# Windowed attention and a feed-forward network on one core: attention's matrix products in groups, values two pairs behind, a fourth buffer of weights

## The chip, the cores and the metric

The kernel runs on one core of a Trainium2 chip. The metric is the time of one execution in microseconds on the device. Before the change it is 954.46 us, the median of three runs (952.74 to 955.82).

## What is computed

The inputs are q, k and v (8 batches, 8 heads, 576 positions, 64 columns a head) and two weight matrices (512 x 2048 and 2048 x 512), all float32. Each head attends to the last 128 positions with a bias that falls linearly with the distance; then a two-layer network runs over all 4608 tokens:

```
scores = q @ k^T / 8 + slope_h * (-|i - j|),  masked to 0 <= i - j < 128
attn   = softmax(scores);  x = attn @ v          # 4608 x 512 after the heads are joined
h = x @ w_in                                      # 4608 x 2048
g = h if h >= 1, 0 if h <= -1, else (h + 1)^2 / 4
out = g @ w_out                                   # 4608 x 512
```

## The kernel before

The 4608 tokens are cut into 12 chunks of 384 (three blocks of 128). A *pair* is two heads of one chunk, so a chunk has four pairs and the program 48 (`p` = 0 to 47). The first two chunks of attention (pairs 0 to 7) run in float32. From pair 8 on (`p8`) every operand is split into a high and a low float16 half, and each product is made of three: high x high, high x low, low x high.

**Scores of a pair** (`scores_of_pair`, L451). The two heads lie on partitions 0 to 63 and 64 to 127, so a score product uses half the rows of the array (64*128 in the profile), and the two heads' products alternate. Blocks 0 and 1 together are 12 products into two PSUM banks, one for each head; block 2 is a second call with 6 products into two more banks. All of attention shares three banks (`ps_a`). `soften` (L467) then takes the bias and the row minimum on VectorE (L484) and the exponential on ScalarE (L486).

**Weights.** `weights_t` (L507) scales and splits the softmax of one head into float16 (`hl`, L531 and L532) and transposes it with a DMA on the queue of SyncE (L533) into `lu`, which has three buffers.

**Values of a pair** (`values_of_pair`, L558). 24 products (18 in the chunks that begin a batch) multiply `lu` with the split v (`vs`). Each head fills half the output columns (128*64 in the profile). The sum lies in one of the three banks and is split into `xh` on ScalarE (L580) and `xl` on VectorE (L581).

**Feed-forward.** For each of 16 slices of the hidden layer, `layer1` (L597) makes 12 products of 384 columns into one of two banks (`ps_h`). The gate `g` is made on ScalarE and in two halves on VectorE (L607 to L609), then split (`gh` on ScalarE, L616; `gl` on GpSimd, L617). `layer2` (L620) makes 9 products of 512 columns two slices later. These use the whole array (128*128).

**What sets the order.** `segments` (L655 to L724) lists the steps of attention; `emit_attention` (L728) gives them out in step with the slices of the feed-forward of the chunk before, so that attention of chunk c + 1 runs under the feed-forward of chunk c. A scheduler then places each instruction on its engine at build time by priority and by when it holds its inputs ready; each engine runs its list in that order. `behind` (L240) fixes that a step stands after given instructions of its engine: the products of one call are chained with it, but others may stand between them. In the loop from L698, pair p's scores (blocks 0 and 1), scores (block 2), values of pair p - 1, and weights of pair p follow one another.

Of the kernel before, what the change touches and what calls it, by code (L numbers as in the profile page):

```python
# [8 lines left out]
F32 = mybir.dt.float32  # L9
F16 = mybir.dt.float16  # L10
# [10 lines left out]
def windowed_attention_then_ffn(  # L21
# [26 lines left out]
    P = 128  # L48
# [3 lines left out]
    NQB = 3  # L52
    CH = NQB * P
    NCHUNK = NT // CH
    NP = NCHUNK * NPAIR
# [5 lines left out]
    X = mybir.AxisListType.X  # L61

    LIGHT = 2

    const = ctx.enter_context(tc.tile_pool(name="const", bufs=1))
    wp = ctx.enter_context(tc.tile_pool(name="wp", bufs=1))
# [2 lines left out]
    ap1 = ctx.enter_context(tc.tile_pool(name="ap1", bufs=1))  # L69
# [170 lines left out]
    def behind(instructions, f):  # L240

        with ExitStack() as stack:
            for i in instructions:
                stack.enter_context(tc.issue_after(i))
            f()


    pair = {}
    head = {}
    xn = {}  # L250
# [2 lines left out]
    softened, scored_at = {}, {}  # L253
    lo_rows = [slice(0, D), slice(D, P)]
# [5 lines left out]

    late = []
    vns = {}

    def load_first(p):

        n = f"_{p}"
        if p < 2:
            qr = ap1.tile([P, CH], F32, name="qr" + n, tag=("qr", "ql")[p])
        else:
            if p == 2:  # L270
                late.append(wp.tile([P, 2, CH], F32, name="qr_23", tag="wo5"))
            qr = late[0][:, p - 2]
        kr = k_0[p // 2][:, p % 2]
        pair[p] = dict(qr=qr, ql=qr, kr=kr)
        DMA.dma_start(qr, q[p * P:(p + 1) * P, :CH])
        DMA.dma_start(kr, k[p * P:(p + 1) * P, :CH])

    def load_qk(p):

        c, g = divmod(p, NPAIR)  # L280
        if c == 0 or c >= LIGHT:
            return
        n = CH + before(c) * P
        st = pair.setdefault(p, {})
        qr = st["qr"] = ap1.tile([P, CH], F32, name=f"qr_{p}", tag="qr")
        DMA.dma_start(qr, q[g * P:(g + 1) * P, c * CH:(c + 1) * CH])
        kr = st["kr"] = ap1.tile([P, CH + P], F32, name=f"kr_{p}", tag=("kl", "kk")[p % 2])
        DMA.dma_start(kr[:, :n], k[g * P:(g + 1) * P, (c + 1) * CH - n:(c + 1) * CH])
# [127 lines left out]

    def prepare_q(p):
        if p >= NPAIR:
            ql = pair[p]["ql"] = ap1.tile([P, CH], F32, name=f"ql_{p}", tag="ql")
            S.activation(ql, pair[p]["qr"], AF.Copy, scale=qscale[:, p % NPAIR:p % NPAIR + 1])  # L420

    def split_v(p):
# [28 lines left out]
    def scores_of_pair(p, blks):  # L451
        c = p // NPAIR
        t = pair[p]["h"]
        pts = [bank(f"s_{2 * p + j}_{blks[0]}").rearrange("r (m w) -> r m w", w=2 * P) for j in range(2)]
        last = []
        for n, i in enumerate(blks):
            c0, k0 = window(c, i)
            for s, (a, b) in enumerate(((0, 0), (0, 1), (1, 0))):
                for j, r in ((1, lo_rows[1]), (0, lo_rows[0])):
                    behind(last, lambda: last.append(  # L460
                        T.matmul(pts[j][:, n, c0:], t[r, a, i * P:(i + 1) * P], t[r, b, CH + k0:CH + k0 + 2 * P - c0],  # L461
                                 start=(s == 0), stop=(s == 2)).ins))
                    last = last[-1:]
        for j in range(2):
            softened[p] = soften(2 * p + j, blks, pts[j])

# [40 lines left out]
    def weights_t(m):  # L507

        ep = head[m]["ep"]
        if m < LIGHT * H:  # L510
            pt = bank(f"p_{m}")[:, :CH].rearrange("r (i w) -> r i w", w=P)
            for i in range(NQB):
                T.transpose(pt[:, i, :], ep[:, i, :], ident)
            lu = head[m]["lu"] = ap1.tile([P, 2 * NQB, P], F32, name=f"lu_{m}", tag="lu", bufs=3)
            own = lu[:, 1::2, :]
            ga = S.copy(own, pt)
            G.affine_select(out=lu[:, 0::2, :], in_=own, pattern=[[0, NQB], [-1, P]],
                            base=0, channel_multiplier=1, compare_op=ALU.is_gt, fill=0.0)
            gg = G.affine_select(out=own, in_=own, pattern=[[0, NQB], [1, P]],
                                 base=0, channel_multiplier=-1, compare_op=ALU.is_ge, fill=0.0)  # L520
            done_t[m] = [head[m]["held"].ins, ga.ins, gg.ins]
            return
        lu = head[m]["lu"] = ap1.tile([P, 2, 2 * NQB, P], F16, name=f"lu_{m}", tag="lu", bufs=3)
        hl = ap1.tile([P, 2, NQB, 2 * P], F16, name=f"hl_{m}", tag="ep", bufs=2)
        z, rc = head[m]["z"], head[m]["rc"]
        lone = 1 - before(m // H)
        if lone:
            G.memset(hl[:, :, 0, :P], 0.0)
        for i in range(NQB):
            c0 = P if i < lone else 0  # L530
            S.activation(hl[:, 0, i, c0:], z[:, i, c0:], AF.Copy, scale=rc[:, i:i + 1])  # L531
            V.scalar_tensor_tensor(hl[:, 1, i, c0:], z[:, i, c0:], rc[:, i:i + 1], hl[:, 0, i, c0:], ALU.mult, ALU.subtract)  # L532
        DMA.dma_start(lu.rearrange("p s i w -> p (s i) w"), hl.rearrange("p s i w -> p (s i w)"), transpose=True)  # L533
# [24 lines left out]
    def values_of_pair(p):  # L558
        c, g = divmod(p, NPAIR)
# [2 lines left out]
        lus = [head.pop(2 * p + j)["lu"] for j in range(2)]  # L562
        px = bank(f"x_{p}")[:, :CH]
        todo = [(i, a, b) for i in [*range(NQB), -1] if i + b0 >= 0 for a, b in ((0, 0), (0, 1), (1, 0))]
        last = []
        for n, (i, a, b) in enumerate(todo):
            q0, q1 = max(i, 0), min(i + 2, NQB)
            first = 2 * i + 1 if i >= 0 else 0
            for j, r in enumerate(lo_rows):
                behind(last, lambda: last.append(  # L570
                    T.matmul(px[r, q0 * P:q1 * P], vs[:, a, i + b0, r], lus[j][:, b, first:first + q1 - q0, :].rearrange("p a w -> p (a w)"),  # L571
                             start=(n == 0), stop=(n == len(todo) - 1), skip_group_check=True).ins))
                last = last[-1:]
# [81 lines left out]
    segments = []  # L655
    ready = [0]
    turned = {}
    M1 = LIGHT * H
    p8 = M1 // 2
# [38 lines left out]
    for p in range(p8, NP):  # L698
        c, g = divmod(p, NPAIR)
        nc_, ng = divmod(p + 5, NPAIR)  # L700
        new = p + 5 < NP
        segments.append([lambda p=p: scores_of_pair(p, (0, 1))])
        if p == p8:
            segments.append([lambda p=p: behind(softened[p], lambda: reach_of(p + 4))])
        if new:
# [4 lines left out]
        if g == NPAIR - 1 and c + 1 < NCHUNK:  # L710
            segments.append([lambda c=c: near_of(c + 1)])
        segments.append([lambda p=p: split_v(p)] + ([lambda p=p: load_all(p + 6)] if p + 6 < NP else []))
        if p > p8:
            segments.append([lambda p=p: values_of_pair(p - 1)])
            if g == 0:
                ready.append(len(segments))
# [3 lines left out]
        if p + 1 < NP:  # L720
            segments.append([lambda p=p: split_qk(p + 1)])
        segments.append([lambda p=p: weights_t(2 * p + 1)])
    segments.append([lambda: values_of_pair(NP - 1)])
    ready.append(len(segments))  # L724
    assert len(ready) == NCHUNK + 1
    at = [0]
# [94 lines left out]
    for i, ops in enumerate(ffn):  # L821
        c, r = divmod(i, STEPS)
# [37 lines left out]
```

## Time and profile before

| | |
|---|---|
| median of three runs | 954.46 us (952.74 to 955.82) |
| the profiled execution | 954.13 us |
| its span, first to last instruction | 952.4 us |
| mean granted TensorE clock | 0.988 of full speed |
| TensorE busy | 932.2 us, 98% |
| VectorE busy | 707.2 us, 74% |
| ScalarE busy | 662.6 us, 70% |
| GpSimd busy | 231.3 us, 24% |
| chain of work that ended last | TensorE 88%, VectorE 5%, ScalarE 4% |

PE in the profile is TensorE's matrix products, PEld its loading of the stationary operand, DVE VectorE, ACT ScalarE, POOL GpSimd and SP SyncE. Products are pipelined: the next starts before the last one has ended, so the distance from start to start tells what a product costs, and the length of a row does not. A row of the timeline with "x12" is twelve instructions of one line that follow one another without others between.

### The profile page before, as it was taken

How to read it: one execution, taken by the hardware profiler on the slowest of the kernel's cores; microseconds unless marked ns; L12 is line 12 of the kernel's file. 1: busy time of each engine (PE TensorE's matmuls, PEld its weight loads, DVE VectorE, ACT ScalarE, POOL GpSimd, SP SyncE). 2: the span in 40 equal slices, each digit the busy share in tenths (PEclk: the TensorE clock that was granted, in tenths of full speed). 3: DMA queues.
4: the chain of work that ended last, by engine and by line, in shares of the span. 5: the costliest groups of instructions: out<-in, count | busy, mean ns of one | idle time of the engine just before them, and what ended most of it. 6: DMA issues, size and time to landing. Idle time of an engine off the chain costs nothing.

```text
span 952.4 us, 17560 instructions
## 1 busy us (share of the span) xinstructions
PE 932.2 (98%) x5941; PEld 488.6 (51%) x5941; DVE 707.2 (74%) x2073; ACT 662.6 (70%) x1668; POOL 231.3 (24%) x328
## 2 busy tenths in 40 slices
PE   8889999999999999999999999999999999999997
PEld 6434554455555555555555555555555555455553
DVE  7799979998877877877877877876786777655332
ACT  6788958888678678667667767766866766655332
POOL 5332311121322222222222222122222221221221
PEclk9699999999999999999999999999999999999999
DMA  8557722535435434633532532443433212411000
GB/s 260 190 189 262 230 62 74 86 87 141 85 67 123 84 59 112 113 65 95 111 85 61 126 81 65 112 93 84 107 88 66 67 35 41 93 34 34 34 1 33
DMA packets 178730, 91.32 MB, mean 96 GB/s; under 512 B 128848, under 2 KB 168016, under 8 KB 178640
## 3 DMA queue, kind: packets, MB, share of 16 engines
q1 hardware_dynamic: 178496, 90.07, 38.8%
q8 instruction: 46, 0.75, 0.3%
q14 instruction: 44, 0.36, 0.1%
q10 hardware_dynamic: 144, 0.13, 0.0%
HBM read 49.28 MB, written 9.44 MB: 62 GB/s over the span
## 4 chain that ended last, share of the span: by engine, by line
PE 88%; DVE 5%; ACT 4%; DMA 1%; issue 1%; POOL 0%; SPq 0%; DVEq 0%; ACTq 0%; POOLq 0%
PE h L600 13%; PE acc L632 12%; PE h L601 12%; PE h L602 12%; PE acc L634 12%; PE acc L633 12%; PE s L461 5%; PE x L571 4%; PE acc L629 2%; PE s L445 1%; PE x L548 1%; ACT z L486 1%; DMA vn<-in_v_dram 1%; ACT raw L183 1%; PE idle L88 1%
## 5 line engine op out<-in xcount | busy, mean ns | idle before, releaser
L617 POOL TENSOR_TENSOR gl<-g,gh 128x384 f16<-128x384 f32 x176 | 175.3, 996 | 553.6 <-ACT gh L616 506.6
L608 DVE SCALAR_TENSOR_TENSOR g<-u,half 128x384 f32<-128x384 f32 x176 | 113.6, 646 | 156.6 <-ACT u L607 151.0
L632 PE MATMUL acc<-wo,gh 128*128 128x512 f16 x528 | 200.9, 380 | 0.0
L633 PE MATMUL acc<-wo,gh 128*128 128x512 f16 x528 | 200.2, 379 | 0.0
L634 PE MATMUL acc<-wo,gl 128*128 128x512 f16 x528 | 198.6, 379 | 0.0
L616 ACT CAST gh<-g 128x384 f16<-128x384 f32 x176 | 89.3, 507 | 149.6 <-DVE g L609 126.7
L486 ACT ACTIVATE z<-z,nmax 128x256 f32<-128x256 f32 (+2 forms) x288 | 137.7, 479 | 37.6 <-DVE nmax L484 36.5
L607 ACT ACTIVATE u<-h,shift,fall 128x384 f32<-128x384 f32 x176 | 116.6, 663 | 59.2 <-PE h L602 58.5
L600 PE MATMUL h<-xh,wi 128*128 128x384 f16 x384 | 125.4, 327 | 1.1 <-DVE g L609 1.1
L600 PE MATMUL h<-x,wi 128*128 128x384 f16 x384 | 125.7, 327 | 0.4 <-DVE r L406 0.4
L601 PE MATMUL h<-x,wi 128*128 128x384 f16 x384 | 125.2, 326 | 0.0
L601 PE MATMUL h<-xl,wi 128*128 128x384 f16 x384 | 125.2, 326 | 0.0
L602 PE MATMUL h<-x,wi 128*128 128x384 f16 x384 | 125.2, 326 | 0.0
L602 PE MATMUL h<-xh,wi 128*128 128x384 f16 x384 | 124.9, 326 | 0.0
L484 DVE CUSTOM_DVE_ANT_0 z<-s,near,z_of 128x256 f32<-128x256 f32 (+2 forms) x240 | 98.9, 459 | 23.7 <-PE s L461 23.4
L609 DVE SCALAR_TENSOR_TENSOR g<-h,gain,g 128x384 f32<-128x384 f32 x176 | 108.1, 614 | 3.0
L532 DVE SCALAR_TENSOR_TENSOR hl<-z,rc,hl 128x256 f16<-128x256 f32 (+1 forms) x240 | 104.4, 492 | 7.8 <-ACT hl L531 7.6
L600 PEld LDWEIGHTS <-wi 128*128 128x128 f16 x768 | 74.9, 98 | 64.5 <-issue 11.7
L601 PEld LDWEIGHTS <-wi 128*128 128x128 f16 x768 | 75.2, 98 | 52.2 <-issue 3.7
L602 PEld LDWEIGHTS <-wi 128*128 128x128 f16 x768 | 75.1, 98 | 49.9 <-DVE g L608 0.2
L531 ACT ACTIVATE hl<-z,rc 128x256 f16<-128x256 f32 (+1 forms) x240 | 98.1, 488 | 3.5 <-DVE rc L496 2.9
L634 PEld LDWEIGHTS <-gl 128*128 128x128 f16 x528 | 51.6, 98 | 63.4 <-issue 1.9
(150 smaller groups left out, 1212.0 us busy)
## 6 DMA issues: line engine op xcount, KB each, us to landing
out_dram<-o SPq DMA_DIRECT2D x35, 256.0 KB, 2.8
raw<-in_moe_w_in_dram SPq DMA_DIRECT2D x16, 512.0 KB, 4.1
raw<-in_moe_w_out_dram SPq DMA_DIRECT2D x16, 512.0 KB, 5.0
vn<-in_v_dram SPq DMA_DIRECT2D x32, 256.0 KB, 3.4
qk<-in_q_dram SPq DMA_DIRECT2D x40, 192.0 KB, 2.4
qk<-in_k_dram SPq DMA_DIRECT2D x28, 256.0 KB, 2.9
vn<-in_v_dram SPq DMA_DIRECT2D x16, 192.0 KB, 3.0
qk<-in_k_dram SPq DMA_DIRECT2D x12, 192.0 KB, 2.8
```

What stands on the lines that cost most here:

```text
L486: b = S.activation(z[:, i, c0:], z[:, i, c0:], AF.Exp, bias=nmax[:, i:i + 1], scale=-1.0, accum_out=sm[:, i, 0:1])
L532: V.scalar_tensor_tensor(hl[:, 1, i, c0:], z[:, i, c0:], rc[:, i:i + 1], hl[:, 0, i, c0:], ALU.mult, ALU.subtract)
L600: T.matmul(ph, wi[fc][:, 0, cc, :], xh, start=(cc == 0), stop=False)
L601: T.matmul(ph, wi[fc][:, 0, cc, :], xl, start=False, stop=False)
L602: T.matmul(ph, wi[fc][:, 1, cc, :], xh, start=False, stop=(cc == NCC - 1))
L607: first = S.activation(u, ph, AF.Relu, bias=shift[c] if c else quarter, scale=fall[c][:, col])
L608: V.scalar_tensor_tensor(g, u, half[c] if c else 0.5, u, ALU.min, ALU.mult)
L609: last = V.scalar_tensor_tensor(g, ph, gain[c][:, col] if c else fall[c][:, col], g, ALU.mult, ALU.max)
L617: G.tensor_tensor(gl, g, gh, ALU.subtract)
L632: T.matmul(a, gh[:, ts], wo[fc][:, 0], start=first, stop=False)
L633: T.matmul(a, gh[:, ts], wo[fc][:, 1], start=False, stop=False)
L634: T.matmul(a, gl[:, ts], wo[fc][:, 0], start=False, stop=last)
```

## The change

From pair 8 on, all products of one call of `scores_of_pair` and `values_of_pair` but the first get a raised priority (`held`). For block 2 the order of the two heads is turned round. From pair 14 on (`TIED`) the values of pair p - 2 stand directly behind the scores (blocks 0 and 1) of pair p and are chained to them; until then values follow their pair by one, as before. `lu` gets a fourth buffer, in the place of the two float32 buffers of q of the early pairs, which become the halves of one tile (`q2`). The count of instructions on each engine is the same.

```diff
+    TIED = 14
...
+    def held(last, f):
+
+        if not last:
+            return f()
+        with tc.high_priority(offset=3000):
+            behind(last, f)
+
...
+    q2 = ap1.tile([P, 2, CH], F32, name="q2", tag="q2")
...
-            qr = ap1.tile([P, CH], F32, name="qr" + n, tag=("qr", "ql")[p])
+            qr = q2[:, p]
...
-        qr = st["qr"] = ap1.tile([P, CH], F32, name=f"qr_{p}", tag="qr")
+        qr = st["qr"] = q2[:, 0]
...
-            ql = pair[p]["ql"] = ap1.tile([P, CH], F32, name=f"ql_{p}", tag="ql")
+            ql = pair[p]["ql"] = q2[:, 1]
...
-                for j, r in ((1, lo_rows[1]), (0, lo_rows[0])):
-                    behind(last, lambda: last.append(
+                for j, r in (((1, lo_rows[1]), (0, lo_rows[0])) if blks[0] == 0 else ((0, lo_rows[0]), (1, lo_rows[1]))):
+                    held(last, lambda: last.append(
...
+        if blks[0] == 0 and p >= TIED:
+            scored_at[p] = last[0]
...
-        lu = head[m]["lu"] = ap1.tile([P, 2, 2 * NQB, P], F16, name=f"lu_{m}", tag="lu", bufs=3)
+        n = m % 4
+        lu = head[m]["lu"] = ap1.tile([P, 2, 2 * NQB, P], F16, name=f"lu_{m}", tag="q2") if n == 3 else \
+            ap1.tile([P, 2, 2 * NQB, P], F16, name=f"lu_{m}", tag="lu", bufs=3)
...
-        last = []
+        last = [scored_at[p + 2]] if p + 2 in scored_at else []
...
-                behind(last, lambda: last.append(
+                held(last, lambda: last.append(
...
         segments.append([lambda p=p: scores_of_pair(p, (0, 1))])
+        if p >= TIED:
+            segments.append([lambda p=p: values_of_pair(p - 2)])
+            if g == 1:
+                ready.append(len(segments))
...
-        if p > p8:
+        if p8 < p < TIED - 1:
             segments.append([lambda p=p: values_of_pair(p - 1)])
...
-    segments.append([lambda: values_of_pair(NP - 1)])
+    segments += [[lambda: values_of_pair(NP - 2)], [lambda: values_of_pair(NP - 1)]]
```

What the built programs make of it is shown at three places of pair 23 and the feed-forward of chunk 4. Names end in a running number of the build, which differs between the two programs.

On TensorE before, one product of the scores of block 2 (`s_47_2`, the pair's second head) stands between the two layers of the feed-forward (`h_4_9` is a slice of the first, `acc_4_0` a sum of the second):

```order
L602 LDWEIGHTS wi9_1085
L602 MATMUL h_4_9_5230<-x_4_3_4593,wi9_1085 128x384
L461 LDWEIGHTS h_23_5159
L461 MATMUL s_47_2_5259<-h_23_5159 128x256
L632 LDWEIGHTS gh_4_7_5137
L632 MATMUL acc_4_0_4852<-wo3_2056,gh_4_7_5137 128x512
```

The other five stand 12 products of the feed-forward later. On TensorE after the change the six stand in one piece; these are the last two of them, and the first product behind:

```order
L470 LDWEIGHTS h_23_5050
L470 MATMUL s_46_2_5196<-h_23_5050 128x256
L470 LDWEIGHTS h_23_5050
L470 MATMUL s_47_2_5197<-h_23_5050 128x256
L613 LDWEIGHTS wi8_1006
L613 MATMUL h_4_8_5214<-x_4_0_3910,wi8_1006 128x384
```

The lone product of the pair's third block is gone from its place.

On TensorE before, the values of pair 22 (`x_22`) begin behind the second layer (`acc_4_2`):

```order
L633 MATMUL acc_4_2_4854<-wo4_2218,gh_4_8_5182 128x512
L634 LDWEIGHTS gl_4_8_5183
L634 MATMUL acc_4_2_4854<-wo4_2218,gl_4_8_5183 128x512
L571 LDWEIGHTS vs_22_5039
L571 MATMUL x_22_5324<-lu_44_5141,vs_22_5039 64x256
```

On TensorE after, the values of pair 21 begin behind the twelfth score of pair 23:

```order
L470 MATMUL s_47_0_5096<-h_23_5050 128x256
L470 LDWEIGHTS h_23_5050
L470 MATMUL s_46_0_5095<-h_23_5050 128x256
L584 LDWEIGHTS vs_21_4714
L584 MATMUL x_21_5130<-lu_42_4743,vs_21_4714 64x256
L584 LDWEIGHTS vs_21_4714
L584 MATMUL x_21_5130<-lu_43_4788,vs_21_4714 64x256
```

The values moved from a place of their own in the feed-forward to the end of the scores of the pair two later.

On VectorE before, the passes over the scores of pair 23 (`z_46`, `z_47`) stand behind both halves of the gate of slices 7 and 8 (`g_4_7`, `g_4_8`):

```order
L609 SCALAR_TENSOR_TENSOR g_4_7_5133<-h_4_7_5119,gain4_4638,g_4_7_5133 128x384
L608 SCALAR_TENSOR_TENSOR g_4_8_5178<-u_4_8_5177,half4_4640 128x384
L609 SCALAR_TENSOR_TENSOR g_4_8_5178<-h_4_8_5164,gain4_4638,g_4_8_5178 128x384
L484 ISA z_46_5218,nmax_46_5219<-s_46_0_5204,near_125,z_of5_4134 128x256
L484 ISA nmax_46_5219 128x1
L484 ISA z_46_5218,nmax_46_5219<-s_46_0_5204,near_125,z_of5_4134 128x256
```

On VectorE after, the two passes of the first head stand between the halves of one gate, that of slice 6 (`g_4_6`):

```order
L621 SCALAR_TENSOR_TENSOR g_4_6_5087<-u_4_6_5086,half4_4674 128x384
L495 ISA z_46_5109,nmax_46_5110<-s_46_0_5095,near_125,z_of5_4026 128x256
L495 ISA nmax_46_5110 128x1
L495 ISA z_46_5109,nmax_46_5110<-s_46_0_5095,near_125,z_of5_4026 128x256
L495 ISA nmax_46_5110 128x1
L622 SCALAR_TENSOR_TENSOR g_4_6_5087<-h_4_6_5073,gain4_4672,g_4_6_5087 128x384
```

The second half of the gate moved behind scores that it does not need.

## Rows read from the trace of the kernel before

**Rows 1.** Page, table of engines: busy us, share of the span, instructions.

```profile
PE 932.2 (98%) x5941; PEld 488.6 (51%) x5941; DVE 707.2 (74%) x2073; ACT 662.6 (70%) x1668; POOL 231.3 (24%) x328
```

**Rows 2.** Table by stretch: stretch, its length, busy us of each engine, clock, DMA.

```profile
core 0: us, PE busy (x) PEld busy (x) DVE busy (x) ACT busy (x) POOL busy (x), PEclk, DMA share, GB/s
...
166.00:250.00 84.00, 82.41 (x585) 43.06 (x584) 75.99 (x227) 71.82 (x193) 18.37 (x24) 1.00 0.46 98
250.00:560.00 310.00, 310.00 (x2082) 161.89 (x2081) 239.62 (x699) 220.16 (x580) 73.86 (x93) 1.00 0.43 91
```

**Rows 3.** Waits from 166 us on: who for whom; total us, times, longest.

```profile
PEld L461 <- issue: 44.8, 120, 0.4
...
PE x L571 <- DMA lu<-hl: 1.6, 1, 1.6
```

**Rows 4.** Timeline of TensorE, one score alone: start us, length us, instructions.

```profile
400.21 0.38 PE L633 MATMUL acc<-wo,gh 128*128 128x512 f16 x1
...
401.72 0.38 PE L634 MATMUL acc<-wo,gl 128*128 128x512 f16 x1
402.03 0.28 PE L461 MATMUL s<-h 64*128 64x256 f16 x1
...
402.42 0.33 PE L601 MATMUL h<-x,wi 128*128 128x384 f16 x1
...
404.04 0.33 PE L602 MATMUL h<-x,wi 128*128 128x384 f16 x1
```

**Rows 5.** Timeline of TensorE, five scores.

```profile
411.22 0.33 PE L600 MATMUL h<-x,wi 128*128 128x384 f16 x1
...
411.80 0.50 PE L461 MATMUL s<-h 64*128 64x256 f16 x5
...
412.41 0.33 PE L601 MATMUL h<-x,wi 128*128 128x384 f16 x1
```

**Rows 6.** Timeline of TensorE, six scores.

```profile
242.67 0.33 PE L602 MATMUL h<-x,wi 128*128 128x384 f16 x1
242.93 0.50 PE L461 MATMUL s<-h 64*128 64x256 f16 x6
...
243.59 0.38 PE L633 MATMUL acc<-wo,gh 128*128 128x512 f16 x1
```

**Rows 7.** Timeline of TensorE, the 24 value products of a pair.

```profile
415.43 0.38 PE L634 MATMUL acc<-wo,gl 128*128 128x512 f16 x1
415.74 1.18 PE L571 MATMUL x<-lu,vs 128*64 128x256 f16 x24
...
417.03 0.33 PE L601 MATMUL h<-x,wi 128*128 128x384 f16 x1
```

**Rows 8.** Timeline of TensorE, five scores and 24 values behind them.

```profile
210.64 0.38 PE L633 MATMUL acc<-wo,gh 128*128 128x512 f16 x1
210.95 0.50 PE L461 MATMUL s<-h 64*128 64x256 f16 x5
211.38 1.18 PE L571 MATMUL x<-lu,vs 128*64 128x256 f16 x24
...
212.72 0.38 PE L632 MATMUL acc<-wo,gh 128*128 128x512 f16 x1
```

**Rows 9.** Timeline of all engines, a gate's end and the passes over scores.

```profile
405.89 0.62 DVE L609 SCALAR_TENSOR_TENSOR g<-h,gain,g 128x384 f32<-128x384 f32 x1
...
407.00 0.34 PE L600 MATMUL h<-x,wi 128*128 128x384 f16 x1
...
408.32 0.48 DVE L484 CUSTOM_DVE_ANT_0 z<-s,near,z_of 128x256 f32<-128x256 f32 x1
```

**Rows 10.** Timeline of all engines, the tightest bank of the first layer.

```profile
235.72 0.60 DVE L609 SCALAR_TENSOR_TENSOR g<-h,gain,g 128x384 f32<-128x384 f32 x1
...
236.78 0.34 PE L600 MATMUL h<-x,wi 128*128 128x384 f16 x1
```

## Prediction

> **What bounds the kernel now.** I read the page's table of engines first: TensorE is busy 98% of the span, VectorE 74% [rows 1]. A busy share alone does not say that TensorE is the limit, so the table by stretch came next. From 250 to 560 us TensorE is busy 310.00 of 310.00 us at a granted clock of 1.00 (the 2.4 GHz level), while VectorE has nearly a quarter of its time free; in 166 to 250 us VectorE is busy 75.99 of 84 us, so that is the stretch where it could become late [rows 2]. The waits come third: after 166 us TensorE waited once for data, 1.6 us [rows 3].
>
> The Trainium skill (Perfetto Trace Analysis, Identifying the Most-Contended Engine) speaks against stopping here: matmul busy time is a poor measure because matmuls overlap, and the share of weight loading, 51% here, should judge. By it VectorE would be the engine to relieve. That is the first rival below.
>
> So I read the timeline of single products. Eight 512-column products start from 400.21 to 401.72, seven steps of 0.216 us; 384-column ones start from 402.42 to 404.04, ten steps of 0.162 us [rows 4]. Nothing waits between them. Time is lost only where attention's products, on half the array, stand among those of the feed-forward. I call such a stretch a visit and price it as the time from the start of the product before it to the start of the second product after it, less the plain steps of those two:
> - one score product alone: 402.42 - 401.72 = 0.70, less 0.216 and 0.162: 0.32 us [rows 4];
> - five scores: 412.41 - 411.22 = 1.19, less four steps of 0.162: 0.54 us [rows 5];
> - six scores: 243.59 - 242.67 = 0.92, less 0.378: 0.54 us [rows 6];
> - 24 value products: 417.03 - 415.43 = 1.60, less 0.378: 1.22 us [rows 7];
> - five scores and 24 values in one visit: 212.72 - 210.64 = 2.08, less 0.432: 1.65 us [rows 8].
>
> Five and six cost the same, because scores run in twos, one head on each half of the rows, and an odd one pays for its missing partner. So a visit has a fixed price of about 0.21 us (0.32 less one step of 0.11 for a pair), and a lone score pays the fixed price and an empty half.
>
> **The change part by part.** The same products are issued; their places change. I counted the visits in the built order of TensorE, from pair 8 on (all f16 products of attention).
>
> *Scores held together* (`held`): runs of scores fall from 126 to 87, lone ones from 43 to 6. Joining 1 and 5 into 6 saves 0.32 + 0.54 - 0.54 = 0.32 us; some blocks have 192 or 128 columns and save a little less, so I take 0.31. 39 x 0.31 = 12.1 us. Bounds: the fixed price alone, 39 x 0.21 = 8.2; every lone visit whole, 39 x 0.32 = 12.5.
>
> *Values held together*: runs fall from 46 to 41. I price a split like that of a lone score: 5 x 0.32 = 1.6 us (bounds 1.0 and 1.6).
>
> *Values of pair p-2 directly behind the scores of pair p*: seams between scores and values rise from 3 to 34. A seam saves 0.54 + 1.22 - 1.65 = 0.11 us [rows 5, 7, 8]; 31 x 0.11 = 3.4 us. Bounds: nothing, if the turn from row halves to column halves costs as much as leaving and coming back; 31 x 0.21 = 6.5, if it costs nothing. The one such seam in rows 8 is the same pair of forms, so I take its value.
>
> *Order of the two heads in the third block, one tile for both halves of q*: no instruction more; the copy that reads `q2` has the same readers and the same wait as before. Nothing; if the loads of pairs 4 to 7 came later it would show before 166 us, as at most tenths of a us.
>
> *Fourth buffer of weights*: values of p-2 run while the weights of p-1 are already there, so four are alive. The slot is the old place of q, free after pair 7. The transposing DMAs on SP keep their order and their number; each waits for a buffer whose reader now stands earlier in the pair than the next writer. Nothing. If that cover goes, TensorE waits as it did once at the first values, 1.6 us [rows 3].
>
> *Values one pair later*: the first layer of a chunk needs all four pairs. In chunks 5, 6 and 8 the built order leaves 98 rows between the last values and the first layer, against 62 to 64 before, and the end of the program keeps its 62 rows. No wait.
>
> *Stall terms.* From 250 us on the first layer's banks come free long before they are wanted: the gate ends at 405.89 + 0.62 = 406.51, and the group that reuses its bank starts at 411.22, 4.7 us of room [rows 5, 9]. The tightest place is at 236.78, where the gate ended at 235.72 + 0.60 = 236.32, 0.46 us earlier [rows 10]. There, pairs 8 to 13, the order changes too: one more 0.60 us pass of VectorE ahead of a gate would cost 0.14 us, five of them 2.5. I put the stretch at 0 to 3 us and take 0; the wait of 1.6 us may also go.
>
> Sum: 12.1 + 1.6 + 3.4 = 17.1 us. The profiled run took 954.13 us, 1.7 more than its span of 952.4: 954.13 - 17.1 = 937.0. The median of the three runs is 0.33 us above the profiled one, so I forecast 937.3 us.
>
> **The rivals.**
>
> *TensorE is not the limit.* If busy time misleads, VectorE sets the pace and the moved products only open gaps: 954 us. For it: 74% on VectorE, over 90% in 166 to 250 [rows 1, 2]. Against it: the plain steps have no room for a hidden wait [rows 4]. The rule of the Trainium skill quoted above is not borne out by these rows.
>
> *The three banks become the wait.* A joined visit takes all three banks that attention has: two for scores, the third for values. If one is not yet empty at each of the 32 joined visits, and TensorE waits 0.3 us there, 9.6 us of the gain go: 947 us. For it: the Trainium skill (TensorEngine Tiling, PSUM Bottleneck) warns that packing the array speeds up TensorE but not the emptying of its banks. Against it: of the scores that end at 407.00 the fourth pass of VectorE ends at 408.32 + 0.48 = 408.80 [rows 9], 1.8 us later, while the next visit stands 42 products later, 24 x 0.162 + 18 x 0.216 = 7.8 us.
>
> *The gate falls behind the scores: slower.* VectorE's order now has two passes over the scores between the two halves of a gate (`g_4_6`), so that the gate, and the bank of the first layer, hang on the scores of the visit. It ends about 2 x 0.41 + 0.62 = 1.4 us after the scores instead of before them. Where a first-layer group on that bank follows the visit directly, TensorE waits up to 1.4 us. The gain is eaten from 17.1 / 1.4 = 12 such places on, and at 20 of the 32 the time is 937.3 + 28 = 965 us. For it: the new rows on VectorE. Against it: in the place shown, the group on that bank (`h_4_8`) stands 42 products later, and the room is 4.7 us today [rows 5, 9].
>
> *The order built is not the order meant.* It is partly so: six lone scores and five runs of five stay, and the counts above have them in.
>
> **How the numbers follow.** The forecast has 0.84, the banks 0.08, TensorE not the limit 0.04, the gate behind the scores 0.04. The forecast's own range: the fast end is 937.3 less the 1.6 us wait less the 1.7 us by which the fastest run lies under the median, 934.0; the slow end is 937.3 plus 3 us of the tight stretch, plus 1.4 us of run to run spread, plus the 3.4 us if a seam saves nothing, 945.1. What lies beyond is the banks at 947 and the two rivals behind them, 0.16 in all. Range 934 to 945. A difference under 0.3% (2.9 us) is no change that can be told here. Faster 0.92 (forecast and banks), same 0.04, slower 0.04.
>
> **What would show it.** In the profile after: the score line's busy runs in 12s and 6s with no lone ones from pair 14 on; a joined visit of 12 and 24 costs about 1.98 us (0.87 for twelve scores at six steps of 0.11 and 0.21 fixed, plus 1.22, less 0.11); the weight loads of the scores wait for issue about a third less often than 120 times [rows 3]; TensorE's busy time falls by some 17 us and VectorE's stays within 2 us. Wrong would be: any wait of TensorE for VectorE or for a transposed tile that repeats once a pair after 250 us; a joined visit of over 2.1 us; or an end of the first-chunk stretch that is later than before.

## The result, and the profile after

The changed kernel takes 939.62 us (median of four runs, 938.58 to 942.24), the kernel before beside it 955.14 us (952.74 to 957.36). The ratio is 0.9842, with a 95% interval of 0.981 to 0.9874: 15.5 us faster, against 17.1 forecast. The profiled execution took 939.68 us, 14.5 less than that of before, with a span of 938.0 us. Most of the distance to the forecast is one term, that of the stalls. Executions of one kernel differ by up to 4 us, and the mean granted clock with them (the changed kernel has 0.993 at 938.58 us, 0.987 at 942.24), so that no cause is read from 1 or 2 us between medians.

The page's table of engines after the change [rows 1]:

```profile
PE 917.6 (98%) x5941; PEld 493.1 (53%) x5941; DVE 718.9 (77%) x2073; ACT 660.6 (70%) x1668; POOL 223.6 (24%) x328
```

TensorE is busy 14.6 us less, with the same 5941 products, and its share is 98% as before. That share could not have told beforehand that there was anything to gain. VectorE is busy 11.7 us more.

The table by stretch [rows 2], columns as there:

```profile
166.00:250.00 84.00, 81.16 (x589) 43.20 (x587) 78.48 (x232) 70.59 (x190) 17.63 (x24) 1.00 0.46 104
250.00:560.00 310.00, 310.00 (x2141) 167.30 (x2140) 253.44 (x724) 230.59 (x613) 71.30 (x95) 1.00 0.41 93
```

In 250 to 560 us TensorE still has no idle time, and does 2141 products where it did 2082. In 166 to 250 us it is idle 2.84 us, 1.25 more than before, and VectorE is busy 78.48 of 84. The gain is made in the first kind of stretch, the loss in the second.

The waits from 166 us on [rows 3]: who for whom, total us, times, longest.

```profile
PEld L470 <- issue: 30.9, 78, 0.4
...
PE h L613 <- DVE tt L343: 1.8, 1, 1.8
...
PE h L613 <- DVE half L419: 0.6, 1, 0.6
...
PE x L584 <- DVE nmax L495: 0.2, 1, 0.2
```

Score weights wait for issue 78 times instead of 120, about a third less. The one wait for a transposed tile is gone; three for VectorE are new, and none of them repeats once a pair.

A joined visit in the timeline of TensorE (start us, length us, instructions) [rows 5, 7, 8]:

```profile
392.93 0.33 PE L614 MATMUL h<-x,wi 128*128 128x384 f16 x1
393.10 0.33 PE L615 MATMUL h<-x,wi 128*128 128x384 f16 x1
393.35 0.83 PE L470 MATMUL s<-h 64*128 64x256 f16 x12
394.11 1.18 PE L584 MATMUL x<-lu,vs 128*64 128x256 f16 x24
395.23 0.39 PE L645 MATMUL acc<-wo,gh 128*128 128x512 f16 x1
395.45 0.38 PE L646 MATMUL acc<-wo,gh 128*128 128x512 f16 x1
```

It costs 395.45 - 393.10 = 2.35, less 0.162 and 0.216: 1.97 us, where 1.98 was predicted. After 250 us there are 22 visits of 12 and 24, all at 1.98 us but the four that have narrower scores (1.82 us). No lone score is left there (37 before): all of the third blocks, 33 in number, stand as six, at 0.54 us as in [rows 6] (0.46 where they are narrower).

I priced every visit of both traces from 166 us on as the prediction does. Before there are 163 and after 88. Measured by their starts they sum to 113.9 and 99.1 us; by the prices (fixed, per pair of products, per seam, by each visit's own widths) they should sum to 112.6 and 95.5, a difference of 17.1 as predicted. What the sum after has beyond the prices, about 3.5 us, stands at a few places between 209 and 248 us; before, the one wait of 1.6 us stands beyond them. Without these waits the measured sums are 112.3 and 95.6, a difference of 16.7. The two spans differ by 14.4: the visits with their waits give 14.8, and the first float16 score starts 0.6 us later than before (143.84, 143.23).

The largest of them, in the timeline of VectorE and TensorE, at the place that answers to the tight one [rows 10] (in brackets: idle time just before, and what ended it):

```profile
235.91 0.61 DVE L621 SCALAR_TENSOR_TENSOR g<-u,half 128x384 f32<-128x384 f32 x1
...
236.44 0.55 DVE L594 SCALAR_TENSOR_TENSOR xl<-x,xh 128x384 f16<-128x384 f32 x1
...
236.75 0.77 PE L470 MATMUL s<-h 64*128 64x256 f16 x6
...
236.91 0.34 DVE L495 CUSTOM_DVE_ANT_0 z<-s,near,z_of 128x128 f32<-128x128 f32 x1
...
237.17 0.47 DVE L495 CUSTOM_DVE_ANT_0 z<-s,near,z_of 128x256 f32<-128x256 f32 x1
...
237.58 0.67 DVE L396 TENSOR_REDUCE rows<-vn 128x1 f32<-128x512 f32 x1
...
238.18 0.60 DVE L437 SCALAR_TENSOR_TENSOR vs<-vn,s,vs 128x384 f16<-128x384 f32 x1
...
238.70 0.60 DVE L622 SCALAR_TENSOR_TENSOR g<-h,gain,g 128x384 f32<-128x384 f32 x1
...
239.36 0.32 PE L613 MATMUL h<-x,wi 128*128 128x384 f16 x1 [1.84 <-DVE tt L343]
```

Between the two halves of one gate (235.91 and 238.70) stand five other passes, two of them over scores; before the change only the split of the values (`xl`) stood there. VectorE works without a gap from 235.12 us on, so the gate waits for no score here: it stands in a queue. Only when the second half has read its bank can the first layer go on, at 239.36. The waiting instruction is put down to the short `tt` pass, but the gate's end at 239.30 is what it needed. The visit in front of it, at 236.75, comes to 2.16 us over its price, and 1.84 of it is this wait.

The second place is a lone score with a wait of 0.60 us behind it. A gate's second half and the first layer's product behind the visit, before and after:

```profile
221.42 0.61 DVE L609 SCALAR_TENSOR_TENSOR g<-h,gain,g 128x384 f32<-128x384 f32 x1
...
222.81 0.34 PE L600 MATMUL h<-x,wi 128*128 128x384 f16 x1
```

```profile
221.93 0.61 DVE L622 SCALAR_TENSOR_TENSOR g<-h,gain,g 128x384 f32<-128x384 f32 x1
...
222.59 0.32 PE L613 MATMUL h<-x,wi 128*128 128x384 f16 x1 [0.60 <-DVE half L419]
```

The same three passes stand between the halves in both kernels. Before, the gate ended 0.78 us ahead of the product; after, it ends 0.5 us later, while the score in front of the product starts 0.9 us earlier (221.71, 222.60). TensorE came ahead of a VectorE that had not become faster.

At neither place does the gate hang on the scores of a visit, as in the rival. Passes over scores stand between the halves of 21 of the 171 gates from 166 us on before the change, and of 6 after it; behind one of the six TensorE waits, the one at 235.91. The place of pair 23 that the section on the change shows is among the six, and no sign of what the change does to most gates.

### The profile page after: what moved, and what is told of

The parts are those of the page before. It is cut to its first block, busy times and chain, and to the rows that moved or that the text cites. A ratio compares the mean times of both kernels' runs of the same rounds, so it can differ in the third digit from the quotient of the medians.

```text
span 938.0 us, 17601 instructions
## 1 busy us (share of the span) xinstructions
PE 917.6 (98%) x5941; PEld 493.1 (53%) x5941; DVE 718.9 (77%) x2073; ACT 660.6 (70%) x1668; POOL 223.6 (24%) x328
## 4 chain that ended last, share of the span: by engine, by line
PE 82%; DVE 10%; ACT 5%; issue 1%; DMA 1%; POOL 0%; SPq 0%; ACTq 0%; DVEq 0%; POOLq 0%
PE h L613 12%; PE h L614 12%; PE h L615 12%; PE acc L645 11%; PE acc L646 11%; PE acc L647 11%; PE x L584 4%; PE s L470 4%; PE acc L642 3%; ACT z L497 1%; DVE z L495 1%; PE s L454 1%; DVE g L621 1%; PE x L561 1%; DVE g L622 1%
## 5 line engine op out<-in xcount | busy, mean ns | idle before, releaser
L630 POOL TENSOR_TENSOR gl<-g,gh 128x384 f16<-128x384 f32 x176 | 166.9, 948 | 528.1 <-ACT gh L629 495.0
L621 DVE SCALAR_TENSOR_TENSOR g<-u,half 128x384 f32<-128x384 f32 x176 | 113.6, 645 | 139.9 <-ACT u L620 137.9
L545 DVE SCALAR_TENSOR_TENSOR hl<-z,rc,hl 128x256 f16<-128x256 f32 (+1 forms) x240 | 115.9, 533 | 5.3 <-ACT hl L544 5.2
L495 DVE CUSTOM_DVE_ANT_0 z<-s,near,z_of 128x256 f32<-128x256 f32 (+2 forms) x240 | 98.9, 458 | 14.4 <-PE s L470 14.2
```

The source lines that it names most:

```text
L621: V.scalar_tensor_tensor(g, u, half[c] if c else 0.5, u, ALU.min, ALU.mult)
L630: G.tensor_tensor(gl, g, gh, ALU.subtract)
```

## The experiments

"By price" below is the summed price of all visits in a kernel's built order, less that of before. Each ratio is to the kernel before, run beside it on the same chip (medians 953.93 to 954.40 us).

**held_alone: the kernel before with `held` and nothing else.**

```diff
-                    behind(last, lambda: last.append(
+                    held(last, lambda: last.append(
...
-                behind(last, lambda: last.append(
+                held(last, lambda: last.append(
```

> Before, plus the raised priority inside a call of scores and values, and nothing else (values stay one pair behind, three buffers, heads in the old order). The price theory (TensorE is the limit, and what counts is visits in the built order at the prices of rows 4 to 8): the built order has 142 visits instead of 169 and their summed price falls from 116.2 to 107.6 us, so 955.1 - 8.6 = 946.5 us (945 to 948.5). The prediction's own split of the sum, which gave all joined scores and values to the raised priority: 955.1 - 12.1 - 1.6 = 941.4 us. The rival that VectorE sets the pace: 955 us, no change.

Measured: 945.33 us against 954.12, ratio 0.9912 (0.9891 to 0.9933). That is 8.8 us, as by price, and not the 13.7 that the prediction credits to its two `held` terms. After 250 us the trace still has 15 third blocks cut into one and five scores. The wait for the transposed tile is still there:

```profile
PE x L578 <- DMA lu<-hl: 1.7, 1, 1.7
```

**tie_alone: the changed kernel with `behind` in the place of `held`.**

```diff
-                    held(last, lambda: last.append(
+                    behind(last, lambda: last.append(
...
-                held(last, lambda: last.append(
+                behind(last, lambda: last.append(
```

> The changed kernel without the raised priority (products of a call are only chained, as before); values two pairs behind and chained to the scores, fourth buffer. Price theory: 157 visits in the built order, 11 seams, summed price 112.3 us against 116.2: 955.1 - 3.9 = 951.2 us (949.5 to 953). If the place of the values alone brought the gain, whatever the visits: near 940. If neither part does anything alone: 955.

Measured: 950.19 us, ratio 0.9964 (0.9951 to 0.9976), 3.9 us less than before and as by price. Its trace has 2.6 us of waits between 205 and 238 us, inside visits or directly behind them, 1.0 us more than before has. After 250 us 12 lone scores are left in it.

**lag_untied: values of p - 2, held together, but at the old place and not chained to the scores.**

```diff
-        last = [scored_at[p + 2]] if p + 2 in scored_at else []
+        last = []
...
-        if p >= TIED:
-            segments.append([lambda p=p: values_of_pair(p - 2)])
...
+        if p >= TIED:
+            segments.append([lambda p=p: values_of_pair(p - 2)])
```

> The changed kernel, but the values of pair p-2 keep the place in the pair that values had before and are not chained to the scores (lag of two pairs, four buffers, raised priority stay). Price theory: 148 visits, summed price 110.0 us against 116.2 before and 99.1 changed: 955.1 - 6.1 = 949.0 us (947.5 to 951). The prediction's own split, in which the tie is worth the 31 seams alone: 939.6 + 3.4 = 943.0 us.

Measured: 950.66 us, ratio 0.9958 (0.9944 to 0.9972). That is 3.5 us less than before, where the price says 6.1; its trace has some 3 us of waits, nearly as much as the changed kernel, and before has 1.6. Holding together and standing two pairs behind give less together than holding alone gives (8.8). From here to the changed kernel it is 11 us, which the place directly behind the scores and the chain to them bring; this run does not tell the two apart.

**three_buffers: the changed kernel with three buffers of weights.**

```diff
-        n = m % 4
-        lu = head[m]["lu"] = ap1.tile([P, 2, 2 * NQB, P], F16, name=f"lu_{m}", tag="q2") if n == 3 else \
-            ap1.tile([P, 2, 2 * NQB, P], F16, name=f"lu_{m}", tag="lu", bufs=3)
+        lu = head[m]["lu"] = ap1.tile([P, 2, 2 * NQB, P], F16, name=f"lu_{m}", tag="lu", bufs=3)
```

> The changed kernel with the three buffers of weights of before. Price theory: TensorE's built order is the same as the changed kernel's, 94 visits, 99.1 us; if the late transposes are hidden, 939.6 us (938 to 941.5). The rival that the fourth buffer carries the change: the second head's transpose waits for the values of the pair before, TensorE waits for a transposed tile once a pair, at the 1.6 us of the one such wait before 34 x 1.6 = 54 us, 994 us.

Measured: 940.75 us, ratio 0.9863 (0.9839 to 0.9886). The fourth buffer is not needed: no wait for a transposed tile appears. The trace has the 1.84 us wait of the changed kernel, and behind it something that the changed kernel's trace does not have. The table by stretch of this kernel, and of the changed kernel for the second stretch (the last numbers but two are the granted clock):

```profile
234.00:238.00 4.00, 2.88 (x17) 1.19 (x16) 4.00 (x14) 3.48 (x12) 0.00 (x0) 1.00 0.97 142
239.50:242.40 2.90, 2.90 (x11) 1.24 (x10) 2.80 (x10) 2.45 (x8) 2.06 (x3) 0.50 0.29 86
243.00:246.00 3.00, 3.00 (x18) 1.65 (x17) 2.98 (x9) 2.65 (x7) 0.27 (x1) 1.00 0.21 66
```

```profile
239.50:242.40 2.90, 2.90 (x18) 1.58 (x17) 2.88 (x9) 2.45 (x8) 2.14 (x3) 1.00 0.30 90
```

The clock stood at 0.50 (1.2 GHz) for some 3 us, with 11 products in the stretch where the changed kernel does 18 at 1.00 (2.4 GHz). The ten products from 239.4 us on take 1.6 us more than their plain steps. The 1.1 us between the two medians are within the spread of the runs.

**visits_added: the twelve scores of a pair cut in two by a slice of the first layer, from pair 14 on.** The edit also chains that slice between the two halves; this part is not shown.

```diff
-        segments.append([lambda p=p: scores_of_pair(p, (0, 1))])
+        if p < TIED:
+            segments.append([lambda p=p: scores_of_pair(p, (0, 1))])
+        else:
+            segments.append([lambda p=p: scores_of_pair(p, (0,), False)])
+            segments.append([lambda p=p: scores_of_pair(p, (1,), False)])
```

> The changed kernel, with the twelve scores of blocks 0 and 1 of every pair from 14 on cut in two runs of six by a first-layer slice between them. Lag, tie, seams and buffers stay. Price theory: 157 visits instead of 94, summed price 115.9 us against 99.1, so 939.6 + 16.9 = 956.5 us (955 to 959): the whole gain gone with nothing undone but the grouping. Rival: the gain comes from the values' later place or the fourth buffer, by giving the other engines room: near 940 us.

Measured: 954.51 us against 954.40, ratio 1.0006 (0.9993 to 1.0018). Held groups, tied values and the fourth buffer are all still there, and with 63 more visits the whole gain is gone. The built order also cut the third blocks into one and five again, 31 times after 250 us, as in the timeline of TensorE here (L621 to L624 are the first layer, L656 the second):

```profile
406.02 0.38 PE L656 MATMUL acc<-wo,gl 128*128 128x512 f16 x1
406.33 0.28 PE L476 MATMUL s<-h 64*128 64x256 f16 x1
406.54 0.34 PE L621 MATMUL h<-x,wi 128*128 128x384 f16 x1
406.71 0.33 PE L623 MATMUL h<-x,wi 128*128 128x384 f16 x1
...
407.04 0.33 PE L621 MATMUL h<-x,wi 128*128 128x384 f16 x1
407.30 0.50 PE L476 MATMUL s<-h 64*128 64x256 f16 x5
407.73 0.34 PE L623 MATMUL h<-x,wi 128*128 128x384 f16 x1
407.90 0.33 PE L624 MATMUL h<-x,wi 128*128 128x384 f16 x1
```

One score: 406.71 - 406.02 - 0.378 = 0.31 us; the other five: 407.90 - 407.04 - 0.324 = 0.54; as [rows 4, 5] have it. By price the visits cost 16.9 us more than in the changed kernel. Its profiled span is 954.8, 16.8 more, of which 15.8 are the measured visits (with 0.9 us less of waits) and 0.9 a later first float16 score. Between the medians it is 14.9 us, 2.0 less than by price; its profiled execution was one of its longer ones.

**vector_work_added: a row maximum of v taken three times instead of once for pairs 20 to 47, 56 more passes on VectorE.**

```diff
+        for _ in range(3 if p >= 20 else 1):
+            V.tensor_reduce(tops[c][:, g:g + 1], vn, X, ALU.max, apply_absolute_value=True)
```

> The changed kernel, with the maximum over v on VectorE done three times instead of once for pairs 20 to 47: 56 more passes of about 0.60 us, 33.6 us of VectorE. Theory that TensorE is the limit after the change too: the time follows TensorE's built order alone (100 visits, 100.7 us against 99.1), 939.6 + 1.6 = 941.2 us (940 to 945). Rival that VectorE sets the pace now: 939.6 + 33.6 = 973 us.

Measured: 947.13 us, ratio 0.9925 (0.9906 to 0.9945). Neither number. The added passes take 35.7 us in the trace, VectorE's busy time rises by 28.0, and 7.5 come out at the end. In the stretch where TensorE had no idle time, VectorE is busy 14 us more and TensorE is idle 1.6 us:

```profile
250.00:560.00 310.00, 308.38 (x2141) 167.01 (x2138) 267.41 (x748) 226.28 (x597) 72.14 (x95) 1.00 0.42 93
```

Six waits of 0.5 to 1.1 us came in after 250 us (4.4 us in all), the visits in its order are priced 1.6 us higher, and the clock fell as in the run with three buffers, behind the wait that ends at 239.8 us. Most of the work is hidden: VectorE is not the limit, but it is not far behind.

**gates_first: at two places of 200 to 250 us the passes that stood between the halves of a gate, those over scores excepted, put behind it.** `done_g[2, 2]` is the gate of slice 2 of chunk 2; the passes of `rows` (pair 19) and, at the other place, of `hl` (head 25) are held back in the same way.

```diff
-        V.scalar_tensor_tensor(vs[:, 1, :n], f, s_x[c], vs[:, 0, :n], ALU.mult, ALU.subtract)
+        behind(done_g[2, 2][1:] if p == 15 else [], lambda: V.scalar_tensor_tensor(vs[:, 1, :n], f, s_x[c], vs[:, 0, :n], ALU.mult, ALU.subtract))
...
-        V.scalar_tensor_tensor(xl, px, 1.0 / TOP, xh, ALU.mult, ALU.subtract)
+        behind(done_g[2, 2][1:] if p == 12 else [], lambda: V.scalar_tensor_tensor(xl, px, 1.0 / TOP, xh, ALU.mult, ALU.subtract))
```

> The changed kernel, with VectorE's order mended at the two places where TensorE waits longest: the second half of the gate of slice 2 of chunk 2 stands ahead of the maximum over v, the split of v and the split of the values, and that of slice 15 of chunk 1 ahead of two splits of weights. TensorE's built order is the same. Theory that these passes ahead of the gate make the waits: the wait of 1.84 us falls by three passes (0.60 + 0.53 + 0.47 = 1.6 us) to about 0.25, that of 0.60 us goes, 939.6 - 2.2 = 937.4 us. Rival that something else holds the bank, such as the scores themselves or the first layer's evacuation on ScalarE: the waits stay, 939.6 us.

Measured: 939.27 us, ratio 0.9845 (0.9827 to 0.9862): no difference to the changed kernel. The two visits came down from 2.16 to 0.57 us over their prices and from 0.66 to 0.07, so the moved passes did make those waits. Others came, of 0.95 us at 223.6, 0.61 at 228.4 and this one for GpSimd (TensorE's timeline); whether they came for what had been put back is not shown.

```profile
241.10 0.39 PE L649 MATMUL acc<-wo,gl 128*128 128x512 f16 x1 [1.10 <-POOL gl L632]
```

**heads_not_turned: the third block with the heads in the old order.**

```diff
-                for j, r in (((1, lo_rows[1]), (0, lo_rows[0])) if blks[0] == 0 else ((0, lo_rows[0]), (1, lo_rows[1]))):
+                for j, r in ((1, lo_rows[1]), (0, lo_rows[0])):
```

> The changed kernel, with the two heads in the old order in block 2. Price theory: 96 visits in the built order, 99.5 us against 99.1: 940.0 us (938.5 to 941.5). Rival that the turn is what keeps block 2 together on the chip (the second product waits for the other bank): a wait or a lone score back once a pair, 34 x 0.31 = 10.5 us, 950 us.

Measured: 939.51 us, ratio 0.9846 (0.9829 to 0.9864). The turn is worth nothing that can be measured here. Its waits are others again, 1.8 us at the visit of 175.8 for a transposed tile, as before has one, and 1.6 at that of 237.2, in sum about as much. Behind the first the granted clock stood at 0.50 from 178.9 us on for some 3 us.

**vector_lighter: 16 passes of VectorE over the output weights, 11 of them in 166 to 250 us, taken out.** The low halves are then zeros, and the output lacks their share.

```diff
-        V.scalar_tensor_tensor(t[:, 1], f, s_out, t[:, 0], ALU.mult, ALU.subtract)
+        G.memset(t[:, 1], 0.0)
```

> The changed kernel, with one part left out: the low halves of w_out, which VectorE makes between about 145 and 235 us, are set to zero by GpSimd (so the output lacks their share). VectorE loses 16 passes of 0.74 us, 11.8 us, in the stretch where TensorE waits. Theory that VectorE's load there makes the waits, whichever pass stands first: the 3.5 us of waits of the changed kernel go, the built order has 96 visits (99.3 us against 99.1): 939.6 - 3.5 + 0.2 = 936.3 us (935 to 937.5). Rival that single places of a fixed order make them: they stay or move elsewhere, 939 to 940 us.

Measured: 935.92 us against 954.04, ratio 0.9809 (0.9793 to 0.9825). TensorE waits for nothing from 166 us on:

```profile
166.00:250.00 84.00, 84.00 (x590) 44.16 (x589) 73.98 (x233) 73.12 (x200) 19.95 (x28) 1.00 0.50 108
```

With some 8 us of passes gone there the 3.5 us of waits are gone too. So they hang on VectorE in this stretch; whether on its load or on its order this run does not tell.

**low_halves_on_gpsimd: the same passes computed by GpSimd, in two steps.**

```diff
-        V.scalar_tensor_tensor(t[:, 1], f, s_out, t[:, 0], ALU.mult, ALU.subtract)
+        G.tensor_scalar(f, f, s_out, None, ALU.mult)
+        G.tensor_tensor(t[:, 1], f, t[:, 0], ALU.subtract)
```

> The changed kernel with the same 16 passes taken from VectorE, but computed in full by GpSimd in two passes each (scale in place, subtract), about 16 x 2 us = 32 us on an engine that is busy 17.6 of 84 us in that stretch. If VectorE's load makes the waits: 936.3 us, as with the passes left out. Rival that GpSimd then brings the gate's low half late to the second layer: one such pass of 0.95 us queued behind two of 1 us each, a wait of up to 2 us at some of 16 slices, 940 to 950 us.

Measured: 945.68 us, ratio 0.9908 (0.9894 to 0.9923), 10 us above the run that left them out. VectorE did 210 instructions in 74.66 us of the stretch, where without these passes it did 233 in 73.98:

```profile
166.00:250.00 84.00, 77.73 (x540) 40.52 (x541) 74.66 (x210) 69.44 (x189) 48.61 (x44) 1.00 0.45 100
```

Its passes became longer. The timeline of GpSimd and VectorE (line numbers are one higher than in the changed kernel):

```profile
192.69 1.47 POOL L240 TENSOR_TENSOR wo<-wf,wo 128x512 f16<-128x512 f32 x1
193.07 1.51 DVE L379 SCALAR_TENSOR_TENSOR h<-qk,s_k,h 128x384 f16<-128x384 f32 x1
194.14 1.86 POOL L239 TENSOR_SCALAR wf<-wf,s_out 128x512 f32<-128x512 f32 x1
194.50 1.04 DVE L622 SCALAR_TENSOR_TENSOR g<-u,half 128x384 f32<-128x384 f32 x1
195.58 0.62 DVE L623 SCALAR_TENSOR_TENSOR g<-h,gain,g 128x384 f32<-128x384 f32 x1
```

The pass of L379 (0.60 us where GpSimd is quiet) takes 1.51 and ends 0.42 us after GpSimd's. The gate's second half, at 195.58, is as long as always though GpSimd works beside it; it reads `h` from PSUM. The Trainium skill (SBUF — State Buffer, section "SBUF: two separate sides") says that VectorE and GpSimd share a pair of ports to SBUF that one of them holds for a whole instruction while the other is blocked, and that a VectorE pass with two inputs in SBUF meets there a GpSimd pass that reads SBUF. These rows agree: passes stretch by up to the length of the GpSimd pass, and those with an input in PSUM do not.

**paced_earlier: the changed kernel with attention one slice less ahead under the feed-forward of chunk 1.** One number of the due times, so that pairs 8 to 11 meet other gates.

```diff
-            emit_attention(int(now + (end - now) * (r + (4 if c else 7)) / STEPS))
+            emit_attention(int(now + (end - now) * (r + (4 if c > 1 else 6 if c else 7)) / STEPS))
```

> The changed kernel, with the due times of attention's steps under the feed-forward of chunk 1 one slice later (6 instead of 7 added to the slice number), so that the scores of pairs 8 to 11 meet other gates on VectorE. If TensorE's 3.5 us of waits between 200 and 250 us are accidents of which pass of VectorE stands in front of which gate, another pace meets fewer of them: 937 to 938.5 us. If VectorE's load in that stretch makes them whatever the order, as the run with two places mended suggests, they turn up elsewhere: 939.6 us, no difference that can be told.

Measured: 934.79 us (934.50 to 937.04) against 953.93, ratio 0.9801 (0.9787 to 0.9815). Its median is the lowest of the complete kernels: the five runs all lie below the four of the changed kernel, though on another chip, and the intervals of the two ratios overlap (0.9787 to 0.9815 here, 0.981 to 0.9874 there). The stretch and the waits from 166 us on:

```profile
166.00:250.00 84.00, 83.69 (x601) 44.30 (x601) 80.30 (x242) 72.39 (x197) 19.84 (x26) 1.00 0.50 107
```

```profile
PE acc L645 <- ACT o L658: 0.3, 1, 0.3
PE x L584 <- DVE i L355: 0.2, 1, 0.2
```

VectorE is busier in this stretch than in the changed kernel, 80.30 us, and TensorE waits next to nothing. So it is not the load alone that makes the waits. That what decides is which pass stands in front of which gate fits this, but TensorE's order changed too. Between the two profiled executions 2.6 us lie (937.04 and 939.68), of which 2.0 are the visits (97.1 us measured, 99.1 in the changed kernel) and 0.35 an earlier first float16 score. The other 2 us between the medians are not in the traces; the profiled execution was the slowest of the five, with the lowest mean granted clock (0.988; the fastest had 0.995).

**paced_and_gates_first: the edits of gates_first, and two slices less ahead.**

```diff
-            emit_attention(int(now + (end - now) * (r + (4 if c else 7)) / STEPS))
+            emit_attention(int(now + (end - now) * (r + (4 if c > 1 else 5 if c else 7)) / STEPS))
```

> As the run with two places of VectorE's order mended, and in addition the due times under chunk 1 two slices later (5 instead of 7). The built order of TensorE has about as many visits as the changed kernel, at a summed price about 0.5 us lower. If the waits are accidents of order: 936 to 938 us. If the load of VectorE makes them: 939 to 940 us.

Measured: 937.92 us, ratio 0.9836 (0.9819 to 0.9854), on the same chip as the last one. Between 231 and 243 us TensorE waits 1.3 us (twice) for a bank that ScalarE copies and 0.9 us for GpSimd's `gl`. The order forced by hand brought no gain, alone or here; a pace of two slices less without it was not run.

## Why the prediction was right

Forecast 937.3 us, range 934 to 945; measured 939.62. By its own steps:

- *What bounds the kernel.* Right: TensorE's steps, and on them the visits. The run with visits added took back all of the gain by grouping alone, 14.9 us by medians where the price says 16.9. The first rival, that VectorE sets the pace, is out: 28 us more of busy time on it cost 7.5. The start-to-start steps of single products told this; neither busy share did. The Trainium skill's rule that the prediction weighed (Perfetto Trace Analysis, Identifying the Most-Contended Engine) is right that matmul busy time tells little, 98% before and after; weight loading in its place, 51% and 53%, would have led away from the gain.
- *The sum of visits, 17.1 us.* Right: 16.7 us measured in the traces, the waits left out.
- *Its division among the parts.* Wrong. The prediction counted runs in the order of the whole change and put the 39 runs saved (12.1 us) and the five of the values (1.6) down to `held`. Alone it saves 8.8, tied values alone 3.9; the rest, 2.8 us by the medians, comes only with both. The forecast was spared this mistake, since the counts were those of the whole change. With both the trace has no third block in two pieces after 250 us; with `held` alone it has 15, and tied values alone leave 12 lone scores. By the code, the values then leave the third bank early in the pair, and the third block, which needs two, needs not wait to be placed; this reason was not tried by itself.
- *A seam saves 0.11 us.* Right: the joined visit came at 1.97 to 1.98 us. The bound "nothing, if the turn costs as much as leaving and coming back" is out. The Trainium skill (TensorEngine Tiling (Array Packing), Key Properties) says that a change of tiling mode drains TensorE. By that rule a joined visit has three changes where two visits have four, and the measured saving, 0.54 + 1.22 - 1.65 = 0.11, is about a quarter of two fixed prices of 0.21; the rows agree.
- *Stalls taken at nothing (bounds 0 to 3 us).* The term that was mis-sized. In 209 to 248 us 3.5 us came in, and the 1.6 us of before went: 1.9 us net, where the medians fall 1.6 us short of 17.1. The two places make 2.8 of the 3.5. One gate got four more passes between its halves; at the other TensorE came earlier. The tight place was named in the prediction, with "five of them 2.5" us; four more stood there, and the visit came to 2.16 us over its price.
- *Fourth buffer, turned heads: nothing.* Right, 940.75 and 939.51 without them.
- *VectorE's busy time within 2 us.* Wrong, +11.7. The pass that splits the softmax makes nearly all of it. Its groups in the tables by line (busy us, mean ns), before and after:

```profile
L532 DVE SCALAR_TENSOR_TENSOR hl<-z,rc,hl 128x256 f16<-128x256 f32 x216 | 96.8, 500 | 5.4 <-ACT hl L531 5.2
```

```profile
L545 DVE SCALAR_TENSOR_TENSOR hl<-z,rc,hl 128x256 f16<-128x256 f32 x216 | 108.2, 545 | 2.6 <-ACT hl L544 2.6
```

  Sorted by whether a `gl` pass of GpSimd overlaps them, all 240 of these passes (both widths) take 462 ns (201, without) and 647 (39, beside) before, 462 (175) and 725 (65) after. More of them stand beside GpSimd's `gl`, and those stretch as in low_halves_on_gpsimd. After 250 us that cost TensorE nothing; whether it feeds the waits before 250 was not tried by itself.
- *The gate behind the scores* (0.04): did not come. Fewer gates than before have passes over scores between their halves (6, 21), and at the two gates that TensorE waited for VectorE was not waiting for scores. *The three banks* (0.08): one wait for a bank of attention, 0.2 us at 210.5, and 0.3 us between the first two scores of the visit at 236.75 that may be another; none after 250 us at all.
- *A sign of being wrong, the first-chunk stretch.* The first float16 score starts 0.6 us later than before. The mean granted clock of the first 60 us was 0.80 in that execution and 0.83 in the one of before, and in the other profiled kernels the start lies anywhere from 141.6 to 145.5, so this is not shown to come of the change.

## What to carry to other kernels

Where one engine is full and two kinds of work alternate on it, price a change of kind from start-to-start distances (here 0.21 us a visit, 0.11 for an odd product's missing partner), count the changes in the built order, and the sum is good to half a us of 17, waits left out. Parts of such a change do not add: count each part's own built order before crediting it. A new order moves passes on the helpers too, and a faster engine comes sooner to what they hold: read for each buffer that the full engine waits for what now stands in front of its last reader. Here another pace did more than forcing single passes.

## What the runs showed of the hardware

- After a wait of TensorE of about 1.8 us the granted clock fell to 0.50 for some 3 us in three_buffers (at 239.4 us), vector_work_added (240.6) and heads_not_turned (178.9); after the same wait in the changed kernel's trace, and after 1.7 us in that of held_alone, it stayed at 1.00. So a short wait cost its own length nearly once more (1.6 us in three_buffers), or did not; what decides is not shown.
- GpSimd took 1.61 and 1.29 us (mean, in low_halves_on_gpsimd) for the two steps on 128x512 for which VectorE took 0.74 in one, and a VectorE pass beside them grew to 1.51 us from 0.60.
